# A banded attention stage in another order of work within a step

## The chip, the cores and the metric

The kernel runs on one core of one Trainium2 chip. Its time is the device time in microseconds (us) of one execution; the profile shows one execution of its own, and times in it are counted from the span's start. TensorE (PE, with its weight loads as PEld), VectorE (DVE), ScalarE (ACT) and GpSimd (POOL) each work through their own instructions in the order in which they were written; SyncE (SP) issues the transfers. An instruction that has to wait holds up everything that stands behind it on its engine.

## The reference

Inputs are float32: 4 batches, 8 heads, 768 positions, head size 64, 4 sink keys, a window of 128. Attention comes first, then a token mixer and a gated convolution on its output; the change touches attention alone.

```python
scores = scale * np.matmul(q, k.transpose(0, 1, 3, 2))
keep = is_sink | in_window            # key < 4, or 0 <= row - key < 128
scores = np.where(keep, scores, -1000000000.0)
a = np.exp(scores - np.max(scores, axis=-1, keepdims=True))
a = a / (np.sum(a, axis=-1, keepdims=True) + 1e-09)
x = np.matmul(a, v)                   # heads side by side: (4, 768, 512)
theta = x @ w_theta                   # the mixer's first step
zr, zi = x * np.cos(theta), x * np.sin(theta)
...
```

## The kernel before

Rows of queries are taken in 24 groups g of 128 (6 for each of the 4 batches; i is the group's number in its batch), and a group's 8 heads in 4 pairs p. A step t = 4 g + p is one pair of one group, and the attention stage is a loop over 96 + 20 steps. A row sees at most its own block of 128 keys, the block before it and the 4 sink keys, so the first group of a batch (i = 0) has one block and no sinks of its own, and the other five are full.

What a group goes through, by the helper that does it and the step in which it does:

- `qk_transpose` (L396): k and q, as loaded, are transposed on TensorE, four transposes each, and copied from PSUM to kT and qT (L405). TUNE's lk and lq say how many steps before the group's first step; cq and ck say up to which group VectorE makes the copies, after that ScalarE.
- `scores` (L424 for i = 0, L432 for the others): two pairs at once, at even steps, into two PSUM buffers s0 and s1.
- `softmax`: VectorE merges the two blocks (L447) and takes mask and maximum (L449) for one pair in each step; later ScalarE takes the exponentials with their sums (L455), and L459 adds a small constant.
- `normalise` (L467, L469): two steps later VectorE takes the reciprocal, and GpSimd scales two pairs at once ("scale"); `sink_weights` (L524) makes sk, the scaled weights of the sinks.
- `weights_T` (L480): six steps after their scores the weights of two pairs are transposed on TensorE into the one buffer ps_t, copied to pc by ScalarE (L484), and one step later cut by GpSimd into the part of the block before, pp (L491), and that of the own block, pc (L493): the "selections".
- `sink_T` (L535): sk is transposed, s2 steps after the group's last, copied by ScalarE (L541), corrected by VectorE (L545) and spread by GpSimd into blk (L549).
- `attend` (L508): ten steps after its first, a group's values: 32 matmuls of 128 columns in the profile (16 for i = 0) into ps_x; `finish_x` then adds the sinks with one matmul of 512 columns (L558), and ScalarE copies ps_x to uT (L559).
- `split_x` and `theta`: uT is split in two parts, xh by ScalarE (L567) and xl by GpSimd (L569), and twelve matmuls of 512 columns (L101 to L103) make theta of an older group in the steps p = 0 and p = 1; L582 copies it out.

ps_x, theta's ps_h and the warming matmuls of the first steps (L598) all take turns in one PSUM bank, the tag h. Two PSUM buffers of the tag m are shared by the transposes of k, of q and of sk.

Beside this the stage turns the mixer's token weights round in pieces: a load to `late` (L117), ScalarE's L133, GpSimd's L139, VectorE's joins L148, L151 and L154 and transposes L242, and a store to `wTr` and `wTi` (L246). In the first 16 steps the same is done for theta's weights (L97, L98). Loads of k and q (`step_load`) and of v (`step_value`) are issued by SP.

Within a step, ORDER sets which of these comes first on every engine, since nothing else moves an instruction: the loop goes through its names, and a name is either a helper's step or a list of things put off (`later`) that are now due.

```python
for name in ORDER:
    if name in parts:
        parts[name](t, g, p)
    else:
        deferred(name)
```

Names put off are: scale (L469), cut (the selections), xl, tcopy (L484), scopy (L541), slow (L545), sink (L549), fcopy (L559), thcopy (L582), qcopy and kcopy (L405), exp (L455, L459), low (a copy of sink keys) and wcopy (the stores).

Of the kernel before, what the change touches and what calls it, by code (L numbers as in the profile page):

```python
# [16 lines left out]
PSUM = bass.MemoryType.PSUM  # L17
DRAM = bass.MemoryType.DRAM

TUNE = dict(tc=0, xs=0, we=0, low=1, cut=1, xl=0, th=0, fx=0, nrm=0, w0=18, ll=8, lv=4, lq=4, lk=5, e=0, l2=0, ws=2, wp=3, ga=0, gc=1, cq=5, ck=5, OT=20, LT=6, OX=10, s1=0, s2=2, sl=1, ss=0, lf=0, rk=0, pcd=0, WP=6, kt=2, bk=3, bq=3, bv=3, bqT=2, first=2, kw=4)  # L20
ORDER = ("range scale warm sinksT cut xl turn scores attend finish wth value wcopy scopy slow tcopy load "
         "softmax normalise low loads sink exp join sinks k sinkk q split theta qcopy fcopy thcopy fetch kcopy "
         "wturn ").split()

TWO_PI = 6.283185
INV_TWO_PI = 1.0 / (2.0 * math.pi)
# [9 lines left out]
def tile_sink_window_attention__then__token_mix__then__gated_conv(  # L36
# [16 lines left out]
    nc = tc.nc  # L53
    B, H, S, D = q.shape
    P = 128
    NP = H // 2
# [206 lines left out]
    def banded_attention(mixer):  # L263
        with ExitStack() as c0:
# [234 lines left out]
            def attend(g):  # L499
                i = g % NQ  # L500
                x = xs[g] = ps_h.tile([P, NP, P], F32, tag="h", name="ps_x")
                last = ns == 0 or i == 0
                for p in range(NP):
                    pc, pp = pTs[NP * g + p // 2 * 2]
                    parts = [(g, pc)] if pp is None else [(g, pc), (g - 1, pp)]
                    for a, (gv, w) in enumerate(parts):
                        for h in range(2):
                            nc.tensor.matmul(x[h * D:(h + 1) * D, p, :], vn[gv][:, 2 * p + h, :],  # L508
                                             w[:, p % 2 * 2 + h, :], start=(a == 0 and p == 0),
                                             stop=(last and p == NP - 1 and a == len(parts) - 1),  # L510
                                             skip_group_check=True)
                for p in range(0, NP, 2):
                    pTs.pop(NP * g + p)
                if i > 0:
                    vn.pop(g - 1)
# [36 lines left out]
                later("scopy", 0, copy)  # L552

            def finish_x(g):
                b = g // NQ
                x = xs.pop(g)
                if ns and g % NQ:
                    nc.tensor.matmul(x, vss[b], blks.pop(g), start=False, stop=True, skip_group_check=True)  # L558
                later("fcopy", 0, lambda: copier(TUNE['fx'])(uT[:, :, cols(g)], x))  # L559

            def split_x(g):
# [574 lines left out]
```

## Time and profile before

| | us |
|---|---|
| median of 3 runs | 662.92 (662.25 to 663.28) |
| the profiled execution | 663.22 |
| its span | 661.5 |
| TensorE busy in the span | 635.8 (96%) |
| VectorE, ScalarE, GpSimd busy | 477.6, 362.1, 396.8 |

The profile gives for each engine its busy time in a stretch; for each wait the instruction that waited, what released it, and how long; and in a timeline the instructions one after the other. Matmuls overlap in their pipeline and their ends are modelled, so from one matmul's start to the next one's is what an instruction costs in a row of others, not its own duration. In the timeline, and in the counts, a float32 matmul of scores or values stands as two. Where several things had to be waited for, the view names one of them, not always the last.

Attention takes the first 236 us of the span, the token mixer and the convolution the rest.

### The profile page before, as it was taken

How to read it: one execution, taken by the hardware profiler on the slowest of the kernel's cores; microseconds unless marked ns; L12 is line 12 of the kernel's file. 1: busy time of each engine (PE TensorE's matmuls, PEld its weight loads, DVE VectorE, ACT ScalarE, POOL GpSimd, SP SyncE). 2: the span in 40 equal slices, each digit the busy share in tenths (PEclk: the TensorE clock that was granted, in tenths of full speed). 3: DMA queues.
4: the chain of work that ended last, by engine and by line, in shares of the span. 5: the costliest groups of instructions: out<-in, count | busy, mean ns of one | idle time of the engine just before them, and what ended most of it. 6: DMA issues, size and time to landing. Idle time of an engine off the chain costs nothing.

```text
span 661.5 us, 12467 instructions
## 1 busy us (share of the span) xinstructions
PE 635.8 (96%) x4454; PEld 566.9 (86%) x4454; DVE 477.6 (72%) x1187; ACT 362.1 (55%) x1013; POOL 396.8 (60%) x406
## 2 busy tenths in 40 slices
PE   8679999999999999999999999999999999999998
PEld 4457777777877789999999999999989989989997
DVE  4876677777688449546756767766979889889773
ACT  4779898898898776534353444452423333323222
POOL 4699899879969864324343344447836637537330
PEclk9889999999999999999999999999999999999999
DMA  7686697799982460001000010110010110110111
GB/s 165 162 186 144 139 210 156 147 202 177 199 166 59 137 206 3 1 16 49 33 33 32 33 50 33 49 47 2 1 48 1 49 48 1 49 48 1 49 48 49
DMA packets 104335, 53.36 MB, mean 81 GB/s; under 512 B 80593, under 2 KB 96209, under 8 KB 104273
## 3 DMA queue, kind: packets, MB, share of 16 engines
q1 hardware_dynamic: 104272, 52.56, 32.7%
q8 instruction: 35, 0.57, 0.4%
q14 instruction: 28, 0.22, 0.1%
HBM read 41.54 MB, written 11.01 MB: 79 GB/s over the span
## 4 chain that ended last, share of the span: by engine, by line
PE 69%; POOL 13%; DVE 7%; ACT 5%; issue 3%; DMA 2%; SPq 0%; ACTq 0%; POOLq 0%; DVEq 0%
PE ps_y L103 10%; PE ps_y L101 10%; PE ps_y L102 10%; PE ps_x L508 4%; PE ps_o L103 3%; POOL sm L469 3%; DVE acc L1047 3%; PE ps_o L102 3%; PE ps_o L101 3%; PE ps_c L103 3%; PE ps_c L102 3%; PE ps_c L101 3%; POOL pc L493 2%; PE ps_v L101 2%; PE ps_v L102 2%
## 5 line engine op out<-in xcount | busy, mean ns | idle before, releaser
L98 POOL TENSOR_TENSOR zl<-cs,zh 128x512 fp32r<-128x512 f32 x48 | 65.9, 1373 | 95.2 <-ACT zh L97 80.1
L1047 DVE SCALAR_TENSOR_TENSOR acc<-x,cw,acc 128x384 f32<-128x384 f32 x128 | 106.6, 833 | 2.4
L455 ACT ACTIVATE sm<-sm,nm 128x132 f32<-128x132 f32 (+1 forms) x192 | 76.3, 403 | 13.1 <-DVE nm L449 12.6
L98 POOL TENSOR_TENSOR x2l<-x,x2h 128x384 fp32r<-128x384 f32 x32 | 39.3, 1227 | 55.3 <-ACT x2h L97 55.3
L97 ACT CAST zh<-cs 128x512 fp32r<-128x512 f32 x48 | 29.9, 622 | 76.8 <-DVE cs L892 66.5
L101 PE MATMUL ps_y<-wt0h,zh 128*128 128x384 f32 x192 | 68.2, 355 | 0.0
L469 POOL TENSOR_TENSOR sm<-sm,rs 128x512 f32<-128x512 f32 x48 | 55.9, 1164 | 20.3 <-DVE rs L467 12.7
L103 PE MATMUL ps_y<-wt1h,zl 128*128 128x384 f32 x192 | 64.6, 336 | 0.0
L102 PE MATMUL ps_y<-wt1l,zh 128*128 128x384 f32 x192 | 64.5, 336 | 0.0
L103 PE MATMUL ps_y<-wt0h,zl 128*128 128x384 f32 x192 | 64.5, 336 | 0.0
L102 PE MATMUL ps_y<-wt0l,zh 128*128 128x384 f32 x192 | 64.4, 336 | 0.0
L101 PE MATMUL ps_y<-wt1h,zh 128*128 128x384 f32 x192 | 64.4, 336 | 0.0
L447 DVE COPY_PREDICATED ps_s<-upper,ps_s 128x256 f32<-128x256 int32 x80 | 33.7, 422 | 36.8 <-PE ps_s L432 36.3
L449 DVE CUSTOM_DVE_ANT_0 sm<-ps_s,mask 128x132 f32<-128x132 f32 (+1 forms) x192 | 48.9, 291 | 12.2 <-PE ps_s L424 7.4
L98 POOL TENSOR_TENSOR gl<-acc,gh 128x384 fp32r<-128x384 f32 x28 | 33.7, 1204 | 22.4 <-ACT gh L97 22.4
L508 PE MATMUL ps_x<-pc,vn 128*64 128x128 f32 x384 | 38.0, 286 | 8.8 <-ACT th L582 4.3
L97 ACT CAST x2h<-x 128x384 fp32r<-128x384 f32 x32 | 16.4, 513 | 54.7 <-DVE x L1033 54.7
L101 PE MATMUL ps_v<-x2h,held 128*128 128x384 f32 x128 | 43.3, 338 | 0.0
L102 PE MATMUL ps_v<-x2l,held 128*128 128x384 f32 x128 | 43.2, 338 | 0.0
L103 PE MATMUL ps_v<-x2h,held 128*128 128x384 f32 x128 | 43.2, 338 | 0.0
L892 DVE TENSOR_TENSOR cs<-cs,ps_n 128x512 f32<-128x512 f32 x48 | 32.7, 681 | 11.6 <-ACT cs L885 10.2
L432 PE MATMUL ps_s<-kT,qT 64*64 64x196 f32 x640 | 38.3, 350 | 2.6 <-DVE nm L449 2.2
(159 smaller groups left out, 1937.9 us busy)
## 6 DMA issues: line engine op xcount, KB each, us to landing
vn<-in_v_dram SPq DMA_DIRECT2D x24, 256.0 KB
kn<-in_k_dram SPq DMA_DIRECT2D x23, 256.0 KB
qn<-in_q_dram SPq DMA_DIRECT2D x23, 256.0 KB
out_dram<-o SPq DMA_DIRECT2D x23, 256.0 KB
late<-in_moe_w_tok_r_dram SPq DMA_DIRECT2D x24, 192.0 KB
late<-in_moe_w_tok_i_dram SPq DMA_DIRECT2D x24, 192.0 KB
wTr<-wTe SPq DMA_DIRECT2D x24, 96.0 KB
wTi<-wTe SPq DMA_DIRECT2D x24, 96.0 KB
```

What stands on the lines that cost most here:

```text
L97: nc.scalar.copy(dst_h, src)
L98: lo_engine.tensor_tensor(dst_l, src, dst_h.bitcast(F32), ALU.subtract)
L101: nc.tensor.matmul(ps, lhs[0], rhs[0], start=first, stop=False)
L102: nc.tensor.matmul(ps, lhs[0], rhs[1], start=False, stop=False)
L103: nc.tensor.matmul(ps, lhs[1], rhs[0], start=False, stop=last)
L432: nc.tensor.matmul(ps[a:a + QW, h, a:KT + a + QW], qTs[g][d, p, a:a + QW], keys[:, a:KT + a + QW], start=True, stop=True)
L447: nc.vector.copy_predicated(ps[:, :, KT:KT + P], upper.bitcast(I32)[:, None, :].to_broadcast([P, 2, P]), ps[:, :, 0:P])
L449: nc.vector.tensor_tensor_reduce(sm[:, h, p, a:], ps[:, h, P:KT + P - a], m, -SCALE, BIG, ALU.add, ALU.min, nm[:, h, p:p + 1])
L455: nc.scalar.activation(x, x, AF.Exp, bias=nm[:, h, p:p + 1], scale=-1.0, accum_out=rs[:, h, p:p + 1])
L469: later("scale", 0, lambda: nc.gpsimd.tensor_tensor(x, x, r[:, :, :, None].to_broadcast([P, 2, 2, P]), ALU.mult))
L508: nc.tensor.matmul(x[h * D:(h + 1) * D, p, :], vn[gv][:, 2 * p + h, :], w[:, p % 2 * 2 + h, :], start=(a == 0 and p == 0), stop=(last and ...
L1047: nc.vector.scalar_tensor_tensor(a, x2[:, e, z:z + TB], cw[:, e, z:z + 1], a, ALU.mult, ALU.add)
```

## The change

Two things are changed. The names in ORDER stand in another order, and seven numbers in TUNE differ: low 1 to 2, lq 4 to 3, l2 0 to 1, cq 5 to 6, ck 5 to 4, s2 2 to 3 and kt 2 to 4. So q is transposed one step later (in p = 1, behind theta), the sinks' weights too (in p = 3, behind the values), one copy of q goes from ScalarE to VectorE and one of k the other way. And the sinks' matmul goes from `finish_x`, where it closed a group's sum in PSUM, into `attend`, where it opens it. Line numbers after L500 shift by one or two.

```diff
-ORDER = ("range scale warm sinksT cut xl turn scores attend finish wth value wcopy scopy slow tcopy load "
-         "softmax normalise low loads sink exp join sinks k sinkk q split theta qcopy fcopy thcopy fetch kcopy "
-         "wturn ").split()
+ORDER = ("warm cut range slow scale xl scores sink turn tcopy attend wcopy sinksT softmax theta load scopy "
+         "finish join normalise k thcopy sinkk wth loads split exp wturn sinks low q fcopy value qcopy kcopy "
+         "fetch").split()
...
-                last = ns == 0 or i == 0
+                sinks = ns > 0 and i > 0
+                if sinks:
+                    nc.tensor.matmul(x, vss[g // NQ], blks.pop(g), start=True, stop=False, skip_group_check=True)
...
-                                             w[:, p % 2 * 2 + h, :], start=(a == 0 and p == 0),
-                                             stop=(last and p == NP - 1 and a == len(parts) - 1),
+                                             w[:, p % 2 * 2 + h, :], start=(not sinks and a == 0 and p == 0),
+                                             stop=(p == NP - 1 and a == len(parts) - 1),
...
-                b = g // NQ
                 x = xs.pop(g)
-                if ns and g % NQ:
-                    nc.tensor.matmul(x, vss[b], blks.pop(g), start=False, stop=True, skip_group_check=True)
```

TensorE in the steps 10 and 11, before. ps_sk is the sinks' transpose, ps_t that of the weights, ps_s the scores, ps_x the values:

```order
L535 MATMUL ps_sk<-ident,sk 128x128
L480 MATMUL ps_t<-ident,sm 128x128 x4
L432 MATMUL ps_s_93<-kT,qT 64x196 x4
L432 MATMUL ps_s_94<-kT,qT 64x196 x4
L508 MATMUL ps_x<-pc,vn 64x128 x8
L396 MATMUL ps_qk<-ident,kn 128x128 x4
```

And the same work now:

```order
L432 MATMUL ps_s_93<-kT,qT 64x196 x4
L432 MATMUL ps_s_94<-kT,qT 64x196 x4
L480 MATMUL ps_t<-ident,sm 128x128 x4
L510 MATMUL ps_x<-pc,vn 64x128 x8
L537 MATMUL ps_sk<-ident,sk 128x128
L396 MATMUL ps_qk<-ident,kn 128x128 x4
```

The sinks' transpose went from the head of the piece to a place behind the values, and the scores went ahead of the weights' transposes.

ScalarE from one group's copy of values (uT) to the next copy of theta (th), before. pc is the copy of transposed weights, sm an exponential, xh a part of the split:

```order
L559 COPY uT<-ps_x 128x4x128
L455 ACTIVATE sm,rs<-sm,nm 128x132 x2
L459 ACTIVATE rs<-rs,eps 128x2x2
L405 COPY kT<-ps_qk 128x4x128
L133 ACTIVATE wc<-late 128x768
L484 COPY pc<-ps_t 128x512
L413 COPY kT<-kT 128x4x4
L455 ACTIVATE sm,rs<-sm,nm 128x132 x2
L567 CAST xh<-uT 128x512
L405 COPY qT<-ps_qk 128x512
L455 ACTIVATE sm,rs<-sm,nm 128x132 x2
L459 ACTIVATE rs<-rs,eps 128x2x2
L582 COPY th_1617<-ps_h 128x512
```

And the same stretch now:

```order
L558 COPY uT<-ps_x 128x4x128
L543 CAST skr<-ps_sk 128x128
L455 ACTIVATE sm,rs<-sm,nm 128x132 x2
L459 ACTIVATE rs<-rs,eps 128x2x2
L405 COPY kT<-ps_qk 128x4x128
L133 ACTIVATE wc<-late 128x768
L484 COPY pc<-ps_t 128x512
L566 CAST xh<-uT 128x512
L455 ACTIVATE sm,rs<-sm,nm 128x132 x2
L581 COPY th_1606<-ps_h 128x512
L455 ACTIVATE sm,rs<-sm,nm 128x132 x2
L459 ACTIVATE rs<-rs,eps 128x2x2
```

The copy of theta now stands ahead of the second pair of exponentials of its steps, and the copy of q behind them.

GpSimd in two steps of a full group, before (the second selection's pair, scaling, and xl):

```order
L549 TENSOR_TENSOR blk<-skr,bmask 128x512
L524 TENSOR_TENSOR sk<-sm,rs 128x128
L139 TENSOR_SCALAR wc<-wc 128x768
L469 TENSOR_TENSOR sm<-sm,rs 128x2x2x128
L491 AFFINE_SELECT pp<-pc 128x512
L493 AFFINE_SELECT pc<-pc 128x512
L569 TENSOR_TENSOR xl<-uT,xh 128x512
```

And now:

```order
L551 TENSOR_TENSOR blk<-skr,bmask 128x512
L526 TENSOR_TENSOR sk<-sm,rs 128x128
L491 AFFINE_SELECT pp<-pc 128x512
L493 AFFINE_SELECT pc<-pc 128x512
L139 TENSOR_SCALAR wc<-wc 128x768
L469 TENSOR_TENSOR sm<-sm,rs 128x2x2x128
L568 TENSOR_TENSOR xl<-uT,xh 128x512
```

The two selections went ahead of the conversion and the scaling.

## Rows read from the trace of the kernel before

**Rows 1.** Busy time by stretch, us, with instructions in brackets; then TensorE's granted clock.

```profile
14.00:46.00 32.00, 23.07 (x229) 15.35 (x221) 27.13 (x100) 23.78 (x89) 23.48 (x27) 0.89 0.73 167
46.00:236.00 190.00, 180.06 (x1838) 141.33 (x1837) 132.85 (x507) 164.20 (x544) 166.31 (x185) 1.00 0.73 156
75.13:129.41 54.28, 51.67 (x531) 40.68 (x531) 39.85 (x154) 48.24 (x163) 48.76 (x54) 1.00 0.84 176
101.11:129.41 28.30, 26.32 (x270) 20.77 (x266) 20.55 (x77) 24.15 (x82) 26.89 (x30) 1.00 0.82 169
236.00:661.00 425.00, 421.55 (x2346) 403.76 (x2344) 312.73 (x557) 169.31 (x368) 201.80 (x168) 1.00 0.11 38
```

**Rows 2.** Waits of TensorE, 46 to 236 us: total, times, longest.

```profile
PE ps_x L508 <- ACT th L582: 4.3, 9, 0.9
PE ps_x L508 <- issue: 2.2, 2, 1.2
PE ps_x L508 <- POOL xl L569: 1.9, 2, 0.9
PE ps_s L432 <- DVE nm L449: 0.7, 2, 0.5
PE ps_x L508 <- POOL pc L493: 0.4, 1, 0.4
```

**Rows 3.** Timeline, TensorE and ScalarE: start, us, line, tiles, idle before.

```profile
181.09 0.39 PE L103 MATMUL ps_h<-wthh,xl 128*128 128x512 f32 x1
...
181.89 0.40 ACT L455 ACTIVATE sm<-sm,nm 128x132 f32<-128x132 f32 x1 [0.84 <-DVE nm L449]
...
183.01 0.57 ACT L582 COPY th<-ps_h 128x512 f32<-128x512 f32 x1
...
183.68 0.44 PE L508 MATMUL ps_x<-pc,vn 128*64 128x128 f32 x4 [0.94 <-POOL xl L569]
```

**Rows 4.** Timeline of ScalarE near the end of the attention stage.

```profile
224.06 0.59 ACT L582 COPY th<-ps_h 128x512 f32<-128x512 f32 x1 [0.55 <-PE ps_h L103]
...
230.04 1.28 ACT L884 ACT_TABLE_LOAD   x1
```

**Rows 5.** Waits of TensorE in the filling part, 14 to 46 us.

```profile
PE ps_sk L535 <- POOL sk L524: 5.4, 3, 2.2
PE ps_s L432 <- DVE nm L449: 1.5, 1, 1.5
PE ps_t L480 <- ACT pc L484: 1.4, 1, 1.4
```

**Rows 6.** Busy time by stretch, after two of the waits for sk.

```profile
26.00:30.00 4.00, 4.00 (x37) 2.81 (x37) 3.27 (x13) 2.71 (x11) 2.59 (x3) 0.57 0.20 35
36.00:40.00 4.00, 4.00 (x45) 3.16 (x44) 3.18 (x9) 2.81 (x13) 3.93 (x6) 0.57 0.29 71
```

**Rows 7.** Timeline of TensorE in a full group, three neighbours.

```profile
157.62 0.60 PE L396 MATMUL ps_qk<-ident,kn 128*128 128x128 f32 x4
158.06 0.60 PE L480 MATMUL ps_t<-ident,sm 128*128 128x128 f32 x4
158.59 1.23 PE L432 MATMUL ps_s<-kT,qT 64*64 64x196 f32 x16
```

**Rows 8.** Timeline of GpSimd and VectorE in a full group.

```profile
149.74 0.64 POOL L491 TENSOR_SCALAR_AFFINE_SELECT pp<-pc 128x512 f32<-128x512 f32 x1
...
151.05 1.04 POOL L549 TENSOR_TENSOR blk<-skr,bmask 128x512 fp32r<-128x512 f32 x1
...
153.31 1.28 DVE L151 SCALAR_TENSOR_TENSOR wc<-late,wc 128x768 int32<-128x768 int32 x1
...
153.74 1.35 POOL L491 TENSOR_SCALAR_AFFINE_SELECT pp<-pc 128x512 f32<-128x512 f32 x1
```

**Rows 9.** Waits of VectorE in the filling part, 20 to 47 us.

```profile
DVE ps_s L447 <- PE ps_s L432: 3.1, 4, 1.3
```

**Rows 10.** Waits of ScalarE, 46 to 222 us.

```profile
ACT uT L559 <- PE ps_x L558: 11.2, 17, 1.1
```

More of the change, by code (lines that the diff above doesn't have):

```diff
@@ L18 @@
 DRAM = bass.MemoryType.DRAM
-TUNE = dict(tc=0, xs=0, we=0, low=1, cut=1, xl=0, th=0, fx=0, nrm=0, w0=18, ll=8, lv=4, lq=4, lk=5, e=0, l2=0, ws=2, wp=3, ga=0, gc=1, cq=5, ck=5, OT=20, LT=6, OX=10, s1=0, s2=2, sl=1, ss=0, lf=0, rk=0, pcd=0, WP=6, kt=2, bk=3, bq=3, bv=3, bqT=2, first=2, kw=4)
-ORDER = ("range scale warm sinksT cut xl turn scores attend finish wth value wcopy scopy slow tcopy load "
-         "softmax normalise low loads sink exp join sinks k sinkk q split theta qcopy fcopy thcopy fetch kcopy "
-         "wturn ").split()
+TUNE = dict(tc=0, xs=0, we=0, low=2, cut=1, xl=0, th=0, fx=0, nrm=0, w0=18, ll=8, lv=4, lq=3, lk=5, e=0, l2=1, ws=2, wp=3, ga=0, gc=1, cq=6, ck=4, OT=20, LT=6, OX=10, s1=0, s2=3, sl=1, ss=0, lf=0, rk=0, pcd=0, WP=6, kt=4, bk=3, bq=3, bv=3, bqT=2, first=2, kw=4)
+ORDER = ("warm cut range slow scale xl scores sink turn tcopy attend wcopy sinksT softmax theta load scopy "
+         "finish join normalise k thcopy sinkk wth loads split exp wturn sinks low q fcopy value qcopy kcopy "
+         "fetch").split()
 TWO_PI = 6.283185
```

## Prediction

> **What bounds the kernel now.** I read the busy time by stretch first, then TensorE's waits inside the one stretch that is not full, then the rows around the longest of them. The stages after 236 us keep TensorE busy for 421.55 of 425.00 us [rows 1]; the change touches nothing there, so whatever it does happens in the attention stage and then shifts the rest. That stage has two parts. From 46 us, when every kind of work is running, to 236 us, TensorE is busy 180.06 of 190.00 us, so 9.9 us can be won at most without cutting work [rows 1]. Between 14 and 46 us, while the pipeline fills, it is busy 23.07 of 32.00 us at a mean granted clock of 0.89 [rows 1].
>
> In the long part nearly all of the 9.9 us is one wait: the first value matmul of a group (L508) for the single bank with tag h, which it shares with theta's result. Four rows name it: 4.3 behind the copy of theta (L582), 2.2 and 1.9 with other releasers, 0.4 behind a selection [rows 2]. One case read row by row: theta's last matmul starts at 181.09 and lasts 0.39, but its copy starts only at 183.01, because ScalarE stands at an exponential that waited 0.84 us for VectorE; the copy ends at 183.58 and the values start at 183.68 [rows 3]. The view blames GpSimd's xl there, which had long ended; the copy is the true releaser, so I put the 1.9 under L582 too, and the shorter issue wait, of 2.2 - 1.2 = 1.0, likewise. The longer one, of 1.2 at the very end, stands behind the table load for the sine [rows 4].
>
> In the filling part TensorE waits 5.4 us in three places for the sinks' weights of GpSimd (L524), because their transpose stands first in its step, ahead of transposes and scores that are ready; 1.5 us for a softmax, and 1.4 us for a copy of transposed weights that stands behind a wait for a load [rows 5]. After the two longer gaps of the three the granted clock is at half: 0.57 on average from 26 to 30 and from 36 to 40 us, so 2 x 4 x 0.43 = 3.4 us of work at full speed went missing there [rows 6].
>
> **The change part by part.** No matmul, copy or transfer is added or removed; the copies between PSUM and SBUF that change engine (one of q to VectorE, one of k to ScalarE) cancel. Everything is a matter of who stands behind whom.
>
> *Scores ahead of the transposes, sinks' matmul ahead of the values.* Does TensorE pay for the new neighbours? From four k transposes to the next four is 158.06 - 157.62 = 0.44, from four transposes to scores 158.59 - 158.06 = 0.53, so entering scores costs 0.09 [rows 7]. Before and after a group enters scores twice, leaves them twice, and goes in and out of the value shape once. I take nothing; an unseen switch of sinks to values may cost or save some 0.1 a group, 2 us over 20 groups either way, and that stays in the range.
>
> *The sinks' matmul opens the values.* All values of a group now wait for blk (L549), where only the last matmul did. In GpSimd's order blk stands ahead of sk and of the two selections, 0.64 us each, that the second half of the same values needs anyway. So the selections are the later ones, and this costs nothing; if a late sk made blk the last, its 1.04 us would stand in the open, in each group where that happens [rows 8].
>
> *The copy of theta ahead of the next exponentials.* ScalarE now takes L582 when theta ends, not after an exponential that waits for VectorE. In the case above it would start at about 181.6 and end 1.4 us earlier than it did. Between theta's end and the values TensorE now has q's four transposes and four of weights, 0.44 each [rows 7], and the scores, over 0.9 us, against the copy's 0.57: the wait goes entirely. Of 4.3 + 2.2 + 1.9 + 0.4 = 8.8 us, the 1.2 behind the table load stays, so 7.6 can go. What is late next? GpSimd. In the three full groups from 101.11 to 129.41 it is busy 26.89 of 28.30 us, TensorE 26.32 [rows 1]; if GpSimd may not run later than today, only 1.4 of TensorE's 2.0 us can be had. Three such stretches take back 0.6 each, 1.7 in all, and leave 5.9. I take **6.0** for this part; the ends are 3 (GpSimd binds and collides more) and 8.7 (all of it, with the 0.7 us of waits for VectorE and something for later selections).
>
> *Selections ahead of scaling.* A selection feeds the next step's values, while a scaled weight is transposed three steps later, each step a quarter of a group's 54.28 / 6 = 9.05 us: the swap takes time from the one that has it. It is what lets GpSimd run late by the 0.6 us above without TensorE seeing it, so I count no gain of its own.
>
> *Sinks' transpose one step later, q's likewise (s2, lq).* The 5.4 us of TensorE's waits go, and with them, I expect, the half clock. But TensorE alone does not pace this part: VectorE is busy 27.13 of 32.00 us, so at most 4.9 can go [rows 1], of which 3.1 are waits for scores on TensorE [rows 9]. The 1.5 us wait is VectorE's own queue; there the change puts the second softmax ahead of a join and a copy, which helps a little. Between 3.1 and 4.9 I take **4.0**; the low end for the range is 1.5, if GpSimd's splits, also in this part, hold the values instead.
>
> Of SP's queue: loads of k and q now stand ahead of the load of v, which waits for values to end, so they leave no later; I count zero. The copy of the sinks' keys (low), the third load (l2) and the masks' last step (kt) move by a step or two at the start, where no row shows a wait for them; zero as well, inside the bounds of the filling.
>
> **The sum.** 4.0 + 6.0 = 10.0 us. The profiled execution took 663.22 us with a span of 661.5; the median of the three runs is 662.92, 0.3 below it, within their spread. 662.92 - 10.0 = **653** us.
>
> **The rivals.** *GpSimd is the bound.* For: it is the busiest engine next to TensorE, 166.31 of 190.00 us, and its instructions stretch when VectorE works beside them: a selection takes 0.64 at 149.74 and 1.35 at 153.74, where VectorE's join ran for 1.28 us from 153.31 [rows 1, 8]. Closer packing means more such pairs. Against: GpSimd's own waits and an order with more slack. Then the three stretches give 1.4 each, less 0.5 for collisions, 2.7 in all, and the filling 3.1: 662.9 - 5.8 = **657**. The Trainium skill, Perfetto Trace Analysis, section Identifying the Most-Contended Engine, says that matmul busy time is a poor measure of how near TensorE is to its limit, and that the weight loads' share should be read. By that rule TensorE stands at 141.33 of 190.00, 74%, and GpSimd at 88% is the contended one, which is this rival. And SBUF — State Buffer, section Who interferes with whom, says that a VectorE instruction with two inputs in SBUF and a GpSimd instruction that reads SBUF exclude each other for the whole instruction; the two selections agree with it. I stay with TensorE as the bound because its instructions follow one another without a gap in the group of [rows 7], which a share of weight loads does not show.
>
> *ScalarE falls behind, and it ends slower.* The copy of theta now holds the next exponentials until theta ends, and the copy of the values holds others already. ScalarE is busy 48.24 us in the six groups from 75.13, 8.04 a group [rows 1]. It waits for the values up to 1.1 us a group, and 0.55 is what a wait for theta took once [rows 4, 10]. 8.04 + 1.1 + 0.55 = 9.7 against a group's 9.05 now: 0.64 more in 19 groups, 12 us, less 4 of the filling: **671**. It decides if ScalarE reaches both waits early and still has more work between them than TensorE. Against: the waits exist only where ScalarE is early, and at TensorE's own pace, 51.67 / 6 = 8.61 us a group, its 8.04 still fit with 0.57 to spare.
>
> *Nothing comes of it.* The waits for L582 turn into waits for selections, and VectorE paces the filling as now: 662 to 663.
>
> **How the numbers follow.** The forecast has a chance of 0.62 (649 to 656), GpSimd as the bound 0.22 (656 to 661), nothing 0.06, slower 0.10. About 0.2%, 1.3 us, is what a measurement here can tell from no change: faster 0.84, same 0.06, slower 0.10. The range goes from 662.9 - 4.9 - 8.7, less 0.8 for cheaper neighbours, 648.5, to the far side of the GpSimd case, 661.
>
> **What would show it.** Right: no wait of TensorE for sk; a granted clock of 1.00 from 20 to 46 us; the values' waits for L582 under 1 us but for the one at the table load; attention over some 10 us before 236 us; from there the same 425 us. Wrong: the first value matmul or the sinks' matmul waiting for GpSimd in each full group; ScalarE's busy share over 95%; gaps in TensorE before scores; a half clock still there.

## The result and the profile after

| | before | changed |
|---|---|---|
| median, us | 662.66 (662.25 to 663.28, 4 runs) | 656.32 (655.03 to 658.41, 4 runs) |
| profiled execution, us | 663.22 | 656.49 |
| its span, us | 661.5 | 654.8 |

The ratio is 0.9907, with a 95% interval from 0.9879 to 0.9934: faster by some 6.3 us. The forecast was 653, with a range of 648.5 to 661. The time lies in the range, but in the band that I had given to the GpSimd case (656 to 661) and not in the forecast's own (649 to 656). Both halves of the sum have to be looked at, since a total can be nearly right with its parts wrong.

A good ruler for that is the copy of a group's values to uT (L559 before, L558 now), one for each of the 24 groups. Its starts are read from the timeline of ScalarE:

| | before | changed | moved |
|---|---|---|---|
| 3rd copy | 49.32 | 49.44 | +0.1 |
| 6th copy | 77.56 | 76.11 | -1.5 |
| from the 6th to the 23rd, 17 groups | 150.03 | 143.88 | -6.2 |
| from the 23rd to the 24th | 7.56 | 8.25 | +0.7 |
| from the 24th to the end of the span | 426.35 | 426.56 | +0.2 |

So the 17 groups gave what I had forecast for the steady part, 6.0; the filling gave 0 to 1.5 us, depending on where one lets it end, instead of 4.0; and the last group gave 0.7 back. By the second copy, at 39.08 us for 41.04 before, the filling was 2.0 us ahead; it lost that again before the third (see e7).

Busy time by stretch in the changed kernel (columns as in [rows 1]): the filling, a piece of it, and the 17 groups.

```profile
14.00:46.00 32.00, 23.75 (x233) 14.82 (x229) 26.00 (x99) 23.55 (x85) 22.21 (x25) 0.87 0.70 160
24.00:32.00 8.00, 7.00 (x58) 4.47 (x58) 6.55 (x28) 6.67 (x25) 6.88 (x9) 0.57 0.22 46
76.11:219.99 143.88, 143.75 (x1465) 111.36 (x1466) 102.60 (x418) 130.58 (x439) 134.64 (x149) 1.00 0.81 173
```

The same 17 groups in the kernel before:

```profile
77.56:227.59 150.03, 143.23 (x1467) 112.45 (x1466) 108.70 (x417) 131.24 (x440) 132.71 (x149) 1.00 0.79 167
```

TensorE's busy time is the same, 143.2 and 143.75 us; what went is its idle time, from 6.8 to 0.1 us. GpSimd's busy time is nearly the same too (134.64 for 132.71), so its share rose from 88 to 94%. In the filling, against [rows 1], TensorE does hardly more in the 32 us (23.75 for 23.07), and the granted clock is 0.87, not 1.00: a stretch at half rate (0.57 from 24 to 32 us) is still there.

TensorE's waits in the changed kernel, first from 14 to 46 us (the answer to [rows 5]; its other rows are 0.4 us or less), then from 46 to 236 us (the answer to [rows 2]), the whole of that list:

```profile
PE ps_s L432 <- DVE nm L449: 7.1, 5, 3.7
```

```profile
PE ps_x L504 <- ACT th L581: 1.9, 1, 1.9
```

The five rows of [rows 2] are gone but for the one behind the table load, which grew from 1.2 to 1.9 us. The 5.4 us for the sinks' weights in [rows 5] are gone as well, but 7.1 us of scores that wait for the softmax stand in their place, in the same part of the program.

ScalarE's waits, 46 to 222 us:

```profile
ACT uT L558 <- PE ps_x L510: 8.0, 12, 1.8
ACT th L581 <- PE ps_h L103: 6.9, 14, 0.8
```

The second row is new, and it is the edit seen from the other side: ScalarE is now at the copy of theta before theta has ended, 14 times.

### The profile page after: what moved, and what is told of

It is laid out like the page before. It is cut to its first block, busy times and chain, and to the rows that moved or that the text cites. A ratio compares the mean times of both kernels' runs of the same rounds, so it can differ in the third digit from the quotient of the medians.

```text
span 654.8 us, 12500 instructions
## 1 busy us (share of the span) xinstructions
PE 637.2 (97%) x4454; PEld 565.6 (86%) x4454; DVE 472.1 (72%) x1187; ACT 362.3 (55%) x1013; POOL 398.6 (61%) x406
## 4 chain that ended last, share of the span: by engine, by line
PE 82%; DVE 8%; POOL 3%; ACT 2%; DMA 2%; issue 2%; SPq 1%; DVEq 0%; POOLq 0%
PE ps_y L103 10%; PE ps_y L101 10%; PE ps_y L102 10%; PE ps_x L510 5%; PE ps_s L432 4%; PE ps_t L480 4%; PE ps_o L103 3%; DVE acc L1046 3%; PE ps_o L102 3%; PE ps_o L101 3%; PE ps_h L102 3%; PE ps_h L103 3%; PE ps_h L101 3%; PE ps_c L103 3%; PE ps_c L102 3%; PE ps_c L101 3%
## 5 line engine op out<-in xcount | busy, mean ns | idle before, releaser
L449 DVE CUSTOM_DVE_ANT_0 sm<-ps_s,mask 128x132 f32<-128x132 f32 (+1 forms) x192 | 48.7, 291 | 14.4 <-PE ps_t L480 7.5
L469 POOL TENSOR_TENSOR sm<-sm,rs 128x512 f32<-128x512 f32 x48 | 53.1, 1105 | 9.1 <-DVE rs L467 7.9
L101 PE MATMUL ps_h<-wthh,xh 128*128 128x512 f32 x96 | 39.8, 415 | 0.0
```

The costliest lines, as they stand in the source:

```text
L101: nc.tensor.matmul(ps, lhs[0], rhs[0], start=first, stop=False)
L449: nc.vector.tensor_tensor_reduce(sm[:, h, p, a:], ps[:, h, P:KT + P - a], m, -SCALE, BIG, ALU.add, ALU.min, nm[:, h, p:p + 1])
L469: later("scale", 0, lambda: nc.gpsimd.tensor_tensor(x, x, r[:, :, :, None].to_broadcast([P, 2, 2, P]), ALU.mult))
```

## The experiments

Twelve kernels, each timed beside the kernel before on the same chip. In the table "6th to 23rd" is the stretch of 17 groups above, "last" the step from the 23rd copy to the 24th; these are from one profiled execution each.

| run | built on | what | median, us | ratio to before (95%) | 3rd copy | 6th copy | 6th to 23rd | last |
|---|---|---|---|---|---|---|---|---|
| before | | | 662.66 | | 49.3 | 77.6 | 150.0 | 7.6 |
| changed | | | 656.32 | 0.9907 (0.9879, 0.9934) | 49.4 | 76.1 | 143.9 | 8.2 |
| e1 | changed | theta's copy back | 658.61 | 0.9937 (0.9925, 0.9949) | 48.3 | 75.6 | 146.9 | 8.2 |
| e6 | changed | selections back | 659.11 | 0.9945 (0.9933, 0.9958) | 48.1 | 75.2 | 147.4 | 8.2 |
| e7 | changed | scores back | 656.39 | 0.9900 (0.9884, 0.9917) | 46.6 | 74.4 | 144.4 | 9.9 |
| e12 | changed | sinks' matmul closes again | 655.86 | 0.9896 (0.9882, 0.9910) | 48.7 | 75.4 | 144.2 | 8.2 |
| e2 | before | theta's copy ahead | 660.04 | 0.9955 (0.9943, 0.9967) | 49.1 | 76.2 | 148.2 | 7.6 |
| e5 | before | that, and loads of k, q ahead | 658.10 | 0.9933 (0.9920, 0.9945) | 48.6 | 75.7 | 146.8 | 7.6 |
| e3 | before | sinks' transpose later | 662.91 | 0.9994 (0.9985, 1.0002) | 47.8 | 76.2 | 149.8 | 8.2 |
| e9 | before | sinks' value loads later | 662.00 | 0.9988 (0.9980, 0.9997) | 48.1 | 75.8 | 150.1 | 7.6 |
| e10 | before | both of these | 662.36 | 0.9997 (0.9988, 1.0006) | 46.7 | 75.0 | 149.9 | 8.2 |
| e4 | changed | theta's weights a step earlier | 658.22 | 0.9928 (0.9917, 0.9940) | 50.1 | 77.2 | 143.8 | 8.3 |
| e8 | changed | sinks' value loads and first angles later | 651.73 | 0.9837 (0.9824, 0.9850) | 44.7 | 72.8 | 143.8 | 7.4 |
| e11 | changed | GpSimd given 0.64 us more a group | 667.81 | 1.0079 (1.0066, 1.0092) | 49.7 | 79.9 | 153.1 | 7.9 |

A warning for reading it: e1 does the same work in the same order as the changed kernel for its first 40 us, and e12 all but one matmul a group, and the third copies of the three stand at 49.4, 48.3 and 48.7. The filling differs by about 1 us from one execution to the next, so a single profile tells there only of differences well above that; the stretch of 17 groups does not start from that and is much steadier (143.8 to 143.9 in three kernels that do the same in it: the changed one, e4 and e8). Some expectations speak of 19 groups, from the 4th copy on; over these the same three kernels spread from 161.7 to 163.0, so the 17 are used here. The changed kernel's ratio rests on four runs, and its interval touches those of e1, e4 and e6: the parts of the gain are read from the 17 groups, not from the medians.

### Theta's copy put back (e1), and ahead alone (e2)

e1, on the changed kernel:

```diff
-         "finish join normalise k thcopy sinkk wth loads split exp wturn ..."
+         "finish join normalise k sinkk wth loads split exp thcopy wturn ..."
```

> The changed kernel with one thing put back: the copy of theta stands behind the exponentials of its step again. In the changed kernel the 19 full-rate groups from the copy of uT at 58.3 to that at 220.0 us took 161.7 us, before 168.9, a gain of 7.2. If that gain is the copy of theta (my theory), the waits of TensorE's first matmul into the values' bank for L581 come back, 4 to 8 us in all, and the kernel takes 660 to 664. If the gain comes from the other moves (selections ahead of scaling, scores ahead of transposes, the sinks' transpose later), it stays within 1 us of 656.3 and these waits stay under 1 us.

Measured: 658.61, a ratio of 0.9937, between the two cases. The wait is back, 46 to 236 us:

```profile
PE ps_x L504 <- ACT th L581: 4.4, 7, 1.9
```

1.9 of it is the one at the table load, which the changed kernel has too, so 2.5 us came back. The stretch of 17 groups grew from 143.9 to 146.9: theta's copy is worth 3.0 of the 6.2 us, half and not all. (In e1 it stands behind the exponentials but still ahead of fcopy and qcopy, which it followed before, so this prices the exponentials alone.) GpSimd's waits in the 17 groups grew with it:

```profile
POOL sk L526 <- DVE rs L467: 10.2, 9, 1.9
POOL pp L491 <- ACT pc L484: 4.1, 6, 1.1
```

That is 14.3 us, against 7.3 in the changed kernel (3.9 and 3.4, shown below with e6), though the order of GpSimd's own work is the same in both.

e2, on the kernel before:

```diff
-         "softmax normalise low loads sink exp join sinks k sinkk q split theta qcopy fcopy thcopy fetch kcopy "
+         "softmax normalise low loads sink split theta thcopy exp join sinks k sinkk q qcopy fcopy fetch kcopy "
```

> The kernel before with one thing of the change: theta's matmuls and their copy stand ahead of the exponentials of the step. My theory: the 8.4 us of waits behind the copy of theta go down to 1 to 2 (the table load stays) and the kernel takes 656 to 658.5. If the selections ahead of scaling are needed for it, or GpSimd is the bound, the waits turn into waits for the selections L493 or for xl and the kernel takes 660 or more. If exponentials that now stand behind theta hold the transposes of weights, waits of L480 appear and it is slower than 662.7.

The edit takes the split of uT and theta's matmuls along, ahead of q's transposes. Measured: 660.04, at the border of the second case, but for a reason that neither theory had. The waits behind theta's copy did go, down to the 1.2 us of the table load; nothing of GpSimd's took their place. A row that [rows 2] does not have did, from 46 to 222 us:

```profile
PE ps_qk L396 <- DMA kn<-in_k_dram: 3.4, 3, 1.2
```

Three transposes of k, one in each of three batches, now stand and wait for their load.

### With the loads of k and q ahead (e5)

On e2:

```diff
-ORDER = ("range scale warm sinksT cut xl turn scores attend finish wth value wcopy scopy slow tcopy load "
+ORDER = ("range scale warm sinksT cut xl turn scores attend finish load wth value wcopy scopy slow tcopy "
```

> The theta copy ahead alone, as in the run before, and beside it the loads of k and q ahead of theta's weights' and v's loads in SyncE's queue, as in the change. In the run without it, three transposes of k a batch apart waited 1.2, 1.0 and 1.2 us for their load, 3.4 us in all, of a gain of 2.7 us in 168.9. If the order of SyncE's queue is the second half of the change's gain (a part that I had counted at zero), these waits go, the 19 groups take 162.5 to 163.5 us and the kernel 656 to 657.5. If the loads come late because all transfers together do, the waits stay within 1 us of 3.4 and the time at 659 to 661.

Measured: 658.10; the waits for loads of k are gone from the list, which now begins with

```profile
PE ps_s L432 <- DVE nm L449: 1.7, 3, 0.9
```

and the 17 groups take 146.8 for 148.2. So the order on SyncE's queue, which I had counted at zero, is worth 1.4 us once theta's copy is ahead. The kernel before has no wait for a load of k in [rows 2], so there I expect nothing of it; the queue's order alone was not run on that kernel. It does not reach the 162.5 to 163.5 that I wrote for the 19 groups (164.7): something else of the change is missing.

### Selections back behind the scaling (e6)

```diff
-ORDER = ("warm cut range slow scale xl scores ...
+ORDER = ("warm range slow scale cut xl scores ...
```

> The changed kernel with the two selections back behind the scaling on GpSimd. My forecast gave this order no gain of its own, only the room for GpSimd to run late. If GpSimd's order carries part of the gain, the first value matmuls wait for selections (L493, L491) again, 2 to 5 us in all, and the 19 groups take 163.5 to 167 us against 161.7. If not, they take 161.2 to 162.5 and the kernel stays within 1 us of 656.3.

Measured: 659.11, and 147.4 for the 17 groups, 3.5 us more. That covers what was missing. TensorE, 46 to 236 us:

```profile
PE ps_x L510 <- POOL pc L493: 2.6, 6, 0.8
...
PE ps_s L432 <- DVE nm L449: 0.9, 3, 0.5
```

Waits of GpSimd in this kernel, in the 17 groups:

```profile
POOL sk L526 <- DVE rs L467: 7.8, 6, 1.7
POOL sm L469 <- DVE rs L467: 6.8, 6, 1.2
```

in the changed kernel:

```profile
POOL pp L491 <- ACT pc L484: 3.9, 3, 1.3
POOL sk L526 <- DVE rs L467: 3.4, 3, 1.2
```

and in the kernel before, where a row of 0.2 us is left out:

```profile
POOL sm L469 <- DVE rs L467: 7.6, 5, 1.9
POOL sk L524 <- DVE rs L467: 7.1, 3, 2.6
```

Read them one below the other: with the scaling (L469) ahead, GpSimd stands 14.6 or 14.7 us for VectorE's reciprocals; with the selections ahead, 7.3 us in all. The order alone does not make the 7.3, since e1, with the selections ahead, has 14.3. One place, row by row, in e6:

```profile
135.62 0.59 ACT L484 COPY pc<-ps_t 128x512 f32<-128x512 f32 x1
135.88 0.17 DVE L467 RECIPROCAL rs<-rs 128x4 f32<-128x4 f32 x1
136.20 1.04 POOL L469 TENSOR_TENSOR sm<-sm,rs 128x512 f32<-128x512 f32 x1 [1.22 <-DVE rs L467]
137.19 1.35 POOL L491 TENSOR_SCALAR_AFFINE_SELECT pp<-pc 128x512 f32<-128x512 f32 x1
```

and in the changed kernel:

```profile
134.97 0.59 ACT L484 COPY pc<-ps_t 128x512 f32<-128x512 f32 x1
135.24 0.17 DVE L467 RECIPROCAL rs<-rs 128x4 f32<-128x4 f32 x1
135.63 0.64 POOL L491 TENSOR_SCALAR_AFFINE_SELECT pp<-pc 128x512 f32<-128x512 f32 x1 [1.30 <-ACT pc L484]
```

From the start of the copy pc to the first selection it is 1.57 us in e6 (137.19 - 135.62), since the scaling and its reciprocal come between, and 0.66 in the changed kernel. Here GpSimd itself idles as long in both; elsewhere it idles less. Which of the two, the later selections or the idle time, makes more of the 3.5 us these rows don't settle. Nor is all of it a wait of TensorE. The 17 groups of e1, then of e6:

```profile
75.62:222.52 146.90, 144.88 (x1465) 111.54 (x1466) 103.96 (x414) 130.22 (x439) 130.77 (x148) 1.00 0.79 168
75.22:222.59 147.37, 144.98 (x1465) 110.94 (x1466) 104.55 (x421) 130.68 (x438) 131.10 (x149) 1.00 0.81 170
```

TensorE is idle 2.0 and 2.4 us there, for 0.1 in the changed kernel; the other 1.1 and 1.2 us are busy time, more for the same 1465 instructions. What stretched them is not shown.

### Scores back, and the sinks' matmul closing again (e7, e12)

```diff
-         ... slow scale xl scores sink turn tcopy attend wcopy sinksT ...
+         ... slow scale xl sink turn tcopy scores attend wcopy sinksT ...
```

> The changed kernel with the scores back behind the transposes of weights in a step. If the order of the two on TensorE matters in itself, through the softmax that then starts 0.5 us later, waits of scores or of L480 appear and the 19 groups take over 162.7 us against 161.7. If only the queues of the other engines matter, 161.2 to 162.5. In the filling the scores' wait of 3.7 us for the softmax stays in either case, since it is the wait for theta's weights that it hangs on.

> The changed kernel with the sinks' matmul as the last of a group's values again and not the first. I had counted the opening at zero, with 0.1 us a group either way. If so, the stretch from the sixth to the 23rd copy of uT stays within 1.5 us of 143.9 and the kernel at 655 to 658. If the opening gains by itself (a change of shape less) or loses (all values wait for blk), the stretch moves by 2 us or more.

e12's edit, in `attend` of the changed kernel:

```diff
-                if sinks:
-                    nc.tensor.matmul(x, vss[g // NQ], blks.pop(g), start=True, stop=False, skip_group_check=True)
                 for p in range(NP):
...
+                if sinks:
+                    nc.tensor.matmul(x, vss[g // NQ], blks.pop(g), start=False, stop=True, skip_group_check=True)
                 for p in range(0, NP, 2):
```

Measured: 656.39 and 655.86, and 144.4 and 144.2 us for the 17 groups. The two edits that are named first in the change, what comes first on TensorE, are worth 0.5 and 0.4 us there at most, and nothing that the whole time shows. (Over the 19 groups of its expectation e7 took 163.2, over the 162.7 set there, but so did e8, 163.0, with the scores first.) e7's third copy came at 46.6, well ahead of the others. Its wait behind theta's weights stayed, as I had written, now as 3.5 us of weights' transposes. What it lacks is a second one. The changed kernel at its second wait, then its clock and e7's from 44 to 49 us:

```profile
44.56 0.72 PE L432 MATMUL ps_s<-kT,qT 64*64 64x196 f32 x8 [1.90 <-DVE nm L449]
```

```profile
44.00:49.00 5.00, 4.44 (x41) 3.56 (x43) 3.50 (x17) 3.08 (x11) 4.93 (x7) 0.66 1.26 217
44.00:49.00 5.00, 4.85 (x61) 3.68 (x61) 3.13 (x15) 4.42 (x16) 4.93 (x7) 1.00 1.20 226
```

e1 and e12 have that wait too (1.91 and 1.88 us), and the slow stretch behind it; in e7 it is 0.9 us, and the clock stays at 1.00. There the changed kernel lost the 2.0 us that it had won by its second copy. e7 kept most of its lead (37.8 at the second copy, 46.6 at the third), and lost 1.6 at the end, where its last step took 9.9 us.

### The filling: sinks' transpose later alone (e3)

On the kernel before:

```diff
-... s1=0, s2=2, sl=1 ...
+... s1=0, s2=3, sl=1 ...
-ORDER = ("range scale warm sinksT cut xl turn scores attend finish ..."
+ORDER = ("range scale warm cut xl turn scores attend sinksT finish ..."
```

> The kernel before with one thing of the change: the sinks' transpose one step later and behind the values. The 5.4 us of waits for the sinks' weights before 46 us go for certain. If nothing else paces the filling (what I forecast), the third copy of uT comes some 3 us before 49.3 us and the kernel takes 658 to 660. If another wait paces it, the load of theta's weights or the softmax, the scores wait for the softmax instead, as in the changed kernel, the third copy comes within 0.7 us of 49.3, and the time stays at 661.5 to 663.

Measured: 662.91, a ratio of 0.9994. The waits for sk went, as they had to, and the time did not move. What stands there now, 14 to 46 us:

```profile
PE ps_t L480 <- ACT pc L484: 4.2, 3, 2.1
PE ps_s L432 <- DVE nm L449: 2.5, 2, 1.5
```

The third copy came 1.5 us earlier and the sixth 1.4, but the last step is 8.2 us for 7.6 and the 17 groups are unchanged; of a gain of 1.0 us in that profile's span the runs show 0.4 by their ratio, not told from nothing. By the third copy it lies between the two cases, by the time in the second. Of the 4.0 us that I had put on this edit there is no trace in the time. The last step shows the 0.7 us given back: it is 7.6 in e2, e5 and e9, which have the sinks' transpose where it was, and 8.2 or 8.3 in all that have it later, but for e7, e8 and e11. It is the wait behind the table load, 1.2 us before and 1.9 with this edit.

### What holds the filling of the changed kernel (e4, e8)

The timeline of the changed kernel, 10 to 25 us. SPq is the issue of a transfer and how long it held SyncE's queue:

```profile
10.31 4.19 SPq L382 DMA_DIRECT2D vs<-in_v_dram  x6
...
15.67 0.61 SPq L120 DMA_DIRECT2D late<-in_moe_w_theta_dram  x1
...
20.91 0.67 ACT L133 ACTIVATE wc<-late 128x512 f32<-128x512 f32 x1 [3.03 <-DMA late<-in_moe_w_theta_dram]
...
22.57 0.28 DVE L388 TENSOR_TENSOR vr<-vs,vr 32x128 fp32r<-32x128 f32 x1 [2.57 <-ACT vr L387]
...
24.93 1.93 PE L432 MATMUL ps_s<-kT,qT 64*64 64x196 f32 x16 [3.68 <-DVE nm L449]
```

The same L133 in the kernel before:

```profile
19.95 0.67 ACT L133 ACTIVATE wc<-late 128x512 f32<-128x512 f32 x1 [0.68 <-DMA late<-in_moe_w_theta_dram]
```

In the changed kernel, from below: the scores wait 3.68 us for the softmax on VectorE; VectorE stands 2.57 us at the sinks' values (L388) for ScalarE's part of them (L387); that part, with two exponentials ahead of it, stands behind L133, which waits 3.03 us for the second piece of theta's weights; that load was issued at 15.67, because SyncE was held from 10.31 to 14.5 us by six small loads of the sinks' values (L382). e4 asks for the weights a step earlier:

```diff
-... ws=2, ... lf=0, ...
+... ws=1, ... lf=1, ...
```

> The changed kernel with the three later loads of theta's weights issued one step earlier. In the changed kernel ScalarE stood 3.0 us at 17.9 to 20.9 us behind such a load (L133), with exponentials queued behind it, and the scores then waited 3.7 us for the softmax. If this load is what took the filling's gain, that wait shrinks by 1 to 3 us, the third copy of uT comes 1 to 3 us before 49.4 and the kernel takes 653 to 655.5. If VectorE's queue paces the filling, the scores' wait stays and the time is within 0.7 us of 656.3.

Measured: 658.22, not faster than the changed kernel (a ratio of 0.9928 for 0.9907; the intervals overlap). The step was moved, the issue was not:

```profile
16.04 4.71 SPq L120 DMA_DIRECT2D late<-in_moe_w_theta_dram  x2
...
20.91 0.67 ACT L133 ACTIVATE wc<-late 128x512 f32<-128x512 f32 x1 [2.66 <-DMA late<-in_moe_w_theta_dram]
```

It still stands behind the six loads, and now holds the next loads of k and q itself, for 4.71 us. So e8 moves the six instead, and, at the other end of the stage, the first angles behind theta's copy:

```diff
-                    if b == 0 and t == 3:
+                    if b == 0 and t == 5:
...
-            turns = [NT + n for n in (1, 4, 6, 7, 9)]
+            turns = [NT + n for n in (1, 5, 6, 7, 9)]
```

> The changed kernel with two edits at places that the profile tells apart. First, the six small loads of the sinks' values, which hold SyncE's queue from 10.3 to 14.5 us, are issued two steps later, behind the loads of k, q and theta's weights. Theory: in every kernel so far ScalarE got theta's second piece (L133) at 19.8 to 20.9 us, whatever the order of the rest, because its load stands behind those six; then L133 now starts at 16 to 18 us, the scores' wait of 3.7 us goes to under 1.5, the third copy of uT comes at 46.5 to 48 us instead of 49.4. Rival: the transfers or VectorE set the pace and the third copy stays at 48.3 to 49.5. Second, the first angles come a step later, so that the sine's table is loaded behind the copy of theta: the wait of 1.9 us at the last values goes to under 0.4 and the last step takes 6.3 to 6.8 us instead of 8.25. With both by my theory 652 to 654; with the second alone 654 to 655.

Measured: 651.73, 0.9837 of before: the fastest kernel here, by 11 us against before and by 4.6 against the changed one. Its timeline:

```profile
12.10 1.06 SPq L120 DMA_DIRECT2D late<-in_moe_w_theta_dram  x1
...
13.25 4.20 SPq L382 DMA_DIRECT2D vs<-in_v_dram  x6
...
17.75 0.70 ACT L133 ACTIVATE wc<-late 128x512 f32<-128x512 f32 x1
```

The weights are asked for at 12.10 instead of 15.67 us, and L133 starts at 17.75 without a wait. Busy time in the filling, then TensorE's wait for the softmax, 14 to 46 us:

```profile
14.00:46.00 32.00, 24.12 (x286) 15.80 (x282) 28.36 (x111) 26.65 (x97) 26.07 (x29) 1.00 0.75 169
```

```profile
PE ps_s L432 <- DVE nm L449: 6.0, 6, 1.8
```

In the same 32 us TensorE now gets 286 instructions through instead of 233, at a granted clock of 1.00. It is not that it waits less (6.0 for 7.1): the waits are shorter, 1.8 at the longest, and none is followed by a stretch at half rate. The third copy comes 4.8 us earlier, of which 3.3 are left at the sixth; the last step takes 7.4 us for 8.25, a smaller gain than I had hoped for (6.3 to 6.8). At the 23rd copy, ahead of the step in which the angles differ, it is 3.4 us early, and that is the six loads, give or take the 1 us by which fillings differ; the other 1.4 of the 4.8 us between the two spans, in the last step and behind it, I put down to the angles. Neither edit was run alone on the changed kernel.

### The same two causes on the kernel before (e9, e10)

Is it then that load, and not the sinks' weights, that paced the kernel before too? e9 has the first of e8's two edits on the kernel before, e10 that and e3's.

> The kernel before with the six small loads of the sinks' values two steps later, and nothing else. If TensorE's waits for the sinks' weights set the filling of the kernel before, as the prediction has it, these 5.4 us stay and the copy of uT of the sixth group, at 77.56 us before, comes within 0.7 us of that; the time is 662 to 663.5. If the load of theta's weights set it there too, that copy comes 2 us or more earlier and the time is 659 to 661.

> The kernel before with the sinks' transpose later (as in the run of that alone) and the six small loads later. If my forecast for the filling, 3.1 to 4.9 us from the sinks' transpose, failed only because the load of theta's weights held ScalarE, the gain appears here: the copy of uT of the sixth group comes at 73 to 74.5 us (77.56 before, 76.17 with the sinks' transpose alone), and the kernel takes 658 to 660. If VectorE's queue paces the filling as well, it comes at 75.5 to 76.5, and the time is 661.5 to 663.

Measured: 662.00 and 662.36. e9 is faster than before by a hair (0.9988, up to 0.9997); its L133 starts at 18.58 without a wait, and the waits for the sinks' weights stay, 5.6 us. e10, with both stalls taken away, is not measurably faster. So neither the load nor the sinks' weights, nor both, held up the kernel before by more than a hair. The sixth copies, at 75.8 and 75.0, lie outside both cases of their expectations; the profiled executions were among the fastest of each kernel (661.42 and 661.23), so less of it is left in the medians. e10, busy time from 14 to 46 us and TensorE's waits in it:

```profile
14.00:46.00 32.00, 24.05 (x264) 15.71 (x260) 28.66 (x108) 24.97 (x90) 24.56 (x28) 0.95 0.72 172
```

```profile
PE ps_t L480 <- ACT pc L484: 3.4, 4, 1.8
PE ps_s L432 <- DVE nm L449: 3.4, 3, 1.4
```

The transposes of weights wait for the one buffer that ScalarE empties with the copy pc. In the changed kernel this wait is not in the list: there the copy stands ahead of the work on theta's weights in its step (tcopy ahead of wth), and behind it in e10. That this order of ScalarE is what e8 has and e10 lacks is argued from these rows; no run moved it alone, and e8 has the rest of the changed order too.

### More work for GpSimd (e11)

On the changed kernel, in `cut`; the result of the added selection is overwritten by the next one:

```diff
                 def cut(pc, pp):
+                    if p0 == 0:
+                        nc.gpsimd.affine_select(out=pp, in_=pc, pattern=[[0, 4], [-1, P]], base=0, channel_multiplier=1,
+                                                compare_op=ALU.is_gt, fill=0.0)
```

> The changed kernel with one selection more on GpSimd for each full group, 0.64 us of work whose result the next selection overwrites. From the sixth group's copy of uT to the 23rd's, 17 steps between groups of 143.9 us in the changed kernel, GpSimd is busy 134.6: it has 9.2 us idle, and 14 full groups add 9.0. If TensorE alone bounds this stretch and GpSimd has that room, the stretch grows by under 2 us. If GpSimd is the bound (the rival), each addition is paid: 7 to 9 us more. My guess is 2 to 5, since not all of its idle time can be used.

Measured: 667.81, 11.5 us more than the changed kernel. The 17 groups:

```profile
79.92:233.03 153.11, 146.76 (x1465) 111.05 (x1466) 107.45 (x418) 131.71 (x439) 142.85 (x163) 1.00 0.77 164
```

GpSimd has 163 instructions for 149, the 14 added, and the stretch is 153.11 - 143.88 = 9.2 us longer, 0.66 for each. All of it is paid. Its idle time is 10.3 us, no less than the 9.2 of the changed kernel, and the same two rows fill most of it:

```profile
POOL pp L492 <- ACT pc L484: 3.9, 3, 1.3
POOL sk L529 <- DVE rs L467: 3.5, 3, 1.2
```

Three times each, once a batch: the room that I saw lies at the batches' starts. Between two of them, from 83.64 to 130.00 us, the changed kernel has GpSimd busy for 45.46 of 46.36 us, 98%. How the added work reaches TensorE, in the 17 groups of e11:

```profile
DVE wc L148 <- POOL wc L139: 6.5, 7, 1.4
PE ps_s L432 <- DVE nm L449: 3.1, 2, 1.6
```

The first row is not in the changed kernel's list. VectorE now stands at a join of token weights (L148) for GpSimd's conversion, with softmaxes queued behind it: at 128.35 it starts one after such a wait of 1.18 us, and the scores at 131.83 have waited 1.58 us for the softmax. Whether a later join would hide part of the cost was not run.

## Why the prediction came out as it did

**What bounds the kernel.** Right as to the place. All that changed lies in the attention stage, and the rest of the span took 426.35 and 426.56 us. Of the 9.9 us that could be won from 46 us on, 7.0 were: from the third copy to the last it was 185.83 us and is 178.80.

**The copy of theta, 6.0 us.** The mechanism is right: its waits went but for the one at the table load, ScalarE now waits at the copy (14 times, up to 0.8 us), and putting it behind the exponentials again brings back 2.5 us of them. The size is wrong, and the 6.0 for the steady part came out well by luck: other terms, counted at nothing, filled the gap. By e1 the copy is worth 3.0 us; by e2, alone, 1.9, with 3.4 us of new waits for loads.

**Selections ahead of scaling, 0.** This is the step that failed in the steady part: "the swap takes time from the one that has it". I let it only hide GpSimd's lateness, looked at what the selections and the scaling feed, and not at what they wait for. In the place shown the scaling waits for VectorE's reciprocal and the selections behind it start 0.9 us later; e6 prices the order at 3.5 us.

**SyncE's queue, 0.** "So they leave no later" was true, and the question was whether they had to leave earlier. e5 against e2 gives 1.4 us.

The three prices don't add (3.0 + 3.5 is already more than 6.2): undoing one part takes away some of what another gives.

**The filling, 4.0 us.** The second step that failed, and the one that put the total off. The 5.4 us went, and I had asked what is late next only of VectorE's busy time (at most 4.9 us to be had). It was the load that ScalarE's L133 waits for, 0.68 us in the kernel before and 3.03 us now, with the sinks' values that hold VectorE queued behind it: the pipeline came to the same load earlier. When the load came was fixed by SyncE's queue: L133 starts at 20.9 us in the changed kernel and in e4 alike. What was won by the second copy all the same, 2.0 us, went into a second wait for the softmax and the half clock behind it (e7). With the load moved on both, the changed order is 3.4 us ahead at the third copy (44.7 in e8, 48.1 in e9) and 2.9 at the sixth, near the low end of my 3.1 to 4.9; without it neither the moved load nor the sinks' transpose gives more than a hair of time (e9, e10). "And with them, I expect, the half clock" failed for the same reason, and a half clock still there was one of my signs of being wrong: a longer gap, of 3.68 us, was followed by 0.57 from 24 to 32 us. Counted as in the prediction, 7.00 x 0.43 = 3.0 us of work went missing there, an estimate that makes up most of the 4.0.

**Of the parts counted at nothing**, the new neighbours on TensorE and the sinks' matmul that opens the values were right by the 17 groups (e7, e12: 0.5 and 0.4 us). The step of the sinks' transpose cost 0.7 us at the end of the stage, where I had looked for nothing.

**The rivals.** The GpSimd case gave 657 and is nearest in time, but it did not happen as I told it: there TensorE's gain was capped at 2.7 us by a GpSimd that was full, and in fact TensorE's waits went to nothing, while GpSimd's own waits went to half. Its premise was better than I thought, though: e11 shows that GpSimd has no room left in this order of work. The Trainium skill, Perfetto Trace Analysis, section Identifying the Most-Contended Engine, would have TensorE's weight loads read and not its matmul busy time; in the 17 groups they now stand at 111.36 of 143.88 us, 77%, and GpSimd at 94%. For GpSimd e11 agrees with that reading. For TensorE no run tests it: with 143.75 of 143.88 us busy and no wait in the list it looks full at 77% of weight loads, but the same matmuls were busy for 146.76 us in e11, so busy time can hold slack. Which of the two sets the pace of the changed kernel's full groups is open. ScalarE falling behind did not happen: its waits for the values and for theta are 14.9 us from 46 to 222 us, so it is early, not late.

## What to carry to other kernels

A stall that goes is worth nothing until the next thing due at that place has been found, and in a filling pipeline that can be a transfer with a fixed arrival: read back from it to the queue that issues it, and see what holds that queue (here six small loads; moving them, with the angles a step later, gave 4.6 us, some 3.4 of it by the 23rd copy). On an engine with two kinds of work, try the kind whose input is ready ahead of the kind that waits, and price the order by a run: who uses the results did not tell it here, and the engine's waits alone do not either, since they doubled in e1 with its order unchanged. When two engines are above 90%, add a known piece of work to one: what it costs tells whether its idle time is room, and the other engines' waits tell which way the cost takes.

## What the runs showed of the hardware

A gap on TensorE is not always followed by half rate. In e7 the values at the end start after a wait of 1.92 us,

```profile
224.60 0.62 PE L504 MATMUL ps_x<-blk,vr 128*128 128x512 f32 x1 [1.92 <-ACT th L581]
```

and the granted clock from 224 to 229 us is 0.66:

```profile
224.00:229.00 5.00, 4.39 (x36) 3.84 (x37) 1.32 (x3) 0.83 (x2) 0.00 (x0) 0.66 0.01 3
```

In the changed kernel the same matmul follows the same wait of 1.92 us at 225.83, and the clock stays at 1.00:

```profile
225.00:229.00 4.00, 3.17 (x38) 2.70 (x39) 1.32 (x3) 1.45 (x4) 0.00 (x0) 1.00 0.02 4
```

Yet in that kernel the wait of 1.90 us at 44.56 has half rate behind it, as shown with e7. From the first value matmul to the next transposes it was 3.35 us in e7 (225.16 to 228.51) and 1.90 in the changed kernel (226.22 to 228.12): 1.45 of the 1.6 us by which e7's last step was longer. In the kernel before, gaps of 2.16 us (to 25.92) and 1.99 us (to 35.22) had half rate behind them [rows 6], and in e8, with 6.0 us of waits in pieces of up to 1.8, there was none. What tells the two kinds apart is not shown.

The six small loads of the sinks' values, 4 KB each, held SyncE's queue for 4.18, 4.19 and 4.20 us in the kernel before, the changed one and e8, 0.7 us each; a load of k or q of 256 KB held it for 0.38 and 0.53 us at 14.6 and 15.1 us of the changed kernel. Others of 256 KB held it longer (1.28 us at 138.07, and 2.43 at 52.83), so bytes alone do not set it; what does is not shown.

The same instructions of VectorE took 6.1 us less in the 17 groups of the changed kernel (102.60 for 108.70 us), and those of GpSimd 1.9 more (134.64 for 132.71). Which of their instructions met which was not followed further.
